# Taps in longer runs, parameter tables in memory, one addition by transfer

## The chip, the cores and the metric

One core of a Trainium2 chip. The metric is the device time of one execution in microseconds (us); 792.45 is the median of three runs of the kernel before.

## What is computed

Softmax attention with 32 heads of width 16 over 2048 positions, a long convolution whose taps come from a complex state space model, and a gate between the two:

```python
a = softmax(q k^T * 16**-.5) v @ wo              # per head, q, k, v = x @ wqkv
K = einsum("dn,dnl,dn->dl", C, exp(dt*A*l), dt*B).real   # 512 channels, 128 modes, 2048 taps
b = causal_conv(x, K) + x * Dskip
out = g * a + (1 - g) * b                        # g = sigmoid(sum(x * gate_w))
```

## The kernel before

The program of every engine is written out by a planner in Python. It knows a cost for each operation and a landing time for each transfer (`c`, `lat`, and a margin `DMARG` = 1.2 us on transfers), runs a model clock for each engine (`tm`), and lets threads (generators such as `params`, `tables`, `kgen`, `cloads`, `convs`, `projs`, `gate`) put their next operation in when it is ready by that model; a lower number is a higher priority. Each engine then does its list strictly in that order and waits on semaphores where a tile isn't there yet.

**Attention sets the beat.** The 2048 score tiles (128 keys by 512 queries) come in 683 groups of three. TensorE forms a group's scores in one of two PSUM banks (`SC`), ScalarE takes the exponential into `ET` (`ex`, line 949), TensorE multiplies by the values into `OA` (`pv`). A block is one head's 512 queries, 16 quads of four tiles; 32 blocks. Everything else is put in around this.

**VectorE takes tiles over.** In some groups ScalarE does two tiles and VectorE the third by bit arithmetic (`bits`, line 985; `batch`, line 996; tiles `DZ`, `DU`). Four such groups make a set. When sets may be taken is written in constants: the first window `WIN` opens at group 206 with four key positions of a block (`VKT`), the second at group 400 with seven, and none is taken before the mark "tabs" (`DVQ`), which is set when the last table is done; after it each set must find 0.3 us of modelled idle time of VectorE.

**Taps.** `params` makes complex powers of the modes and from them factors for two tables. For each of eight units `w` of 64 channels `tables` makes a left table `AT` (2 x 32 x 64 per mode) and a right table `PL` (2 x 112 x 64), both by doubling: copy a base, then `cmul` (two products and an addition) twice, and for `PL` six products with the factors `FF`. `AT`, `PL` and the eviction target `Ks` have two buffers each; a unit's tables wait for the mark `kg` of the unit two back. `kgen(w)` multiplies the tables on TensorE into the PSUM bank `MB` (2 x 128 matmuls of a 32-wide stationary operand), VectorE evicts to `Ks` (line 1240), and SP stores to `kd` in device memory. `MB` is under a lock that `kgen`, `projs`, `gate`, `convs`, `turn` and `outs` share.

**Convolution.** `cloads` loads for each of 32 channel groups the taps `WT` (four transfers; each partition reads a shifted stretch, in runs of 512 B) and the input `U`; `convs` does 128 matmuls with 32 columns of `WT` as the stationary operand, 16 elements apart; VectorE evicts (`Ys`), `turn` transposes by matmuls with `sel`. After the convolutions `outs` projects and writes out. `PACE` raises the priority of `convs` when they are behind a straight line from group 235 to 620.

Of the kernel before, what the change touches and what calls it, by code (L numbers as in the profile page):

```python
# [28 lines left out]
NPAD = 16  # L29
VB = (S + NPAD) * 16  # L30
# [24 lines left out]
NPL = 2  # L55
NPSEM = 8
# [3 lines left out]
CLAT = "tabs"  # L60
# [23 lines left out]
POW = (1, 2, 4, 8, 16, 32, 48, 256, 512, 1024)  # L84
# [373 lines left out]
def declare(nc, es):  # L458
# [58 lines left out]
    sb("AB", 7 * 2 * D)  # L517
    sb("BS", 4 * 2 * D)
    for m in (4, 8, 512, 1024):
        sb(f"F{m}", 3 * D)  # L520
    sb("FF", 3 * 3 * D)
    for k in range(2):
        sb(f"AT{k}", 2 * 32 * 64)
    for k in range(NPL):
        sb(f"PL{k}", 2 * 112 * 64)
    sb("ct1", 2 * 16 * 64)
# [112 lines left out]
def record(nc, p, B, ins):  # L639
# [426 lines left out]
    def fmul(o, n, x, xk, y, yk, yat=0, conj=False, at=0, t=("pt1", "pt2"), st=2 * D):  # L1066

        o, x, y, t1, t2 = B[o], B[x], B[y], B[t[0]], B[t[1]]
        c1, c2 = dv(2 * n * D), dv(n * D)
        pl = [[1, D]] if n == 1 else [[2 * D, n], [1, D]]  # L1070
        for tb, part in ((t1, 0), (t2, 1)):
# [5 lines left out]
        tt("DVE", lambda: o(at, [[1, D]] if n == 1 else [[st, n], [1, D]]), lambda: t1(0, pl), lambda: t2(D, pl), ALU.subtract, [(t1, 0), (t2, 0)], W, c2)  # L1077
        yield ("DVE", c2)
        if conj:
            op("DVE", lambda v: v.scalar_tensor_tensor(o(at + D, [[1, D]] if n == 1 else [[st, n], [1, D]]), t1(D, pl), -1.0, t2(0, pl), ALU.mult, ALU.subtract),  # L1080
               [(t1, 0), (t2, 0)], W, c=c2)
        else:
            tt("DVE", lambda: o(at + D, [[1, D]] if n == 1 else [[st, n], [1, D]]), lambda: t1(D, pl), lambda: t2(0, pl), ALU.add, [(t1, 0), (t2, 0)], W, c2)

    def factor(o, x, xk, at=0, xat=0, conj=False):

        o, x = B[o], B[x]
        yield ("DVE", .6)
        op("DVE", lambda v: v.tensor_copy(o(at, [[1, 2 * D]] if conj else [[2 * D, 2], [1, D]]), x(xat, [[1, 2 * D]] if conj else [[D, 2], [1, D]])), xk, [(o, at)], c=.6)
        yield ("DVE", .4)  # L1090
        op("DVE", lambda v: v.tensor_scalar(o(at + (2 * D if conj else D), [[1, D]]), x(xat + D, [[1, D]]), -1.0, None, ALU.mult), xk, [(o, at)], c=.36)

    def params():
        LA, AB, ZW, BS = B["LA"], B["AB"], B["ZW"], B["BS"]
# [19 lines left out]
        yield from fmul("BS", 2, "ZW", zk, "L2", key("L2"), at=4 * D, t=("LT1", "LT2"))  # L1114
        yield ("DVE", 1.15)
        op("DVE", lambda v: v.tensor_copy(BS(0, [[1, 4 * D]]), ZW(0, [[1, 4 * D]])), zk, [(BS, 0)], c=1.15)
        for m in (4, 8):
            yield from square(f"L{m}", f"L{m // 2}")
            yield from factor(f"F{m}", f"L{m}", key(f"L{m}"))
        for k, m in enumerate((16, 32)):  # L1120
            yield from square(f"L{m}", f"L{m // 2}")
            yield from factor("FF", f"L{m}", key(f"L{m}"), 3 * D * k)
        yield from fmul("L48", 1, "L16", key("L16"), "L32", key("L32"))
        yield from factor("FF", "L48", [(B["L48"], (0, "m"))], 6 * D)
        sch.mark("B")
        yield from square("LA", "L32", 0, 0)
# [12 lines left out]
        for m in (512, 1024):
            yield from square(f"L{m}", f"L{m // 2}")  # L1140
            yield from factor(f"F{m}", f"L{m}", key(f"L{m}"), conj=True)
        sch.mark("A")

    AT, PL, ct1 = [B["AT0"], B["AT1"]], [B[f"PL{k}"] for k in range(NPL)], B["ct1"]
# [4 lines left out]
    def ones():  # L1149
        yield ("AFTER", "g40")  # L1150
        for k in range(2):
# [7 lines left out]
    def cmul(x, xk, xs, N, o, W, f, fk, fat, m, ch):  # L1159

        n = 2 * m * ch
        c = hv(n)
        at = (N - 2 * m) * ch
        yield ("DVE", c)
        tt("DVE", lambda: ct1(0, [[m * ch, 2], [ch, m], [1, ch]]), lambda: x((N - m) * ch, [[xs, 2], [ch, m], [1, ch]]),
           lambda: f(fat, [[0, 2], [0, m], [1, ch]]), ALU.mult, xk + fk, [(ct1, 0)], c)
        yield ("DVE", c)
        tt("DVE", lambda: o(at, [[xs, 2], [ch, m], [1, ch]]), lambda: x(xs + (N - m) * ch, [[-xs, 2], [ch, m], [1, ch]]),
           lambda: f(fat + D, [[D, 2], [0, m], [1, ch]]), ALU.mult, xk + fk, W, c)
        yield ("DVE", c)  # L1170
        tt("DVE", lambda: o(at, [[xs, 2], [1, m * ch]]), lambda: ct1(0, [[m * ch, 2], [1, m * ch]]), lambda: o(at, [[xs, 2], [1, m * ch]]),
           ALU.add, [(ct1, 0)] + W, W, c)

    def tables():
        AB, BS, FF = B["AB"], B["BS"], B["FF"]
        yield ("AFTER", "A")
        for w in range(8):
            at, pl, d0 = AT[w % 2], PL[w % NPL], CH * w
            if w >= 2:
                yield ("AFTER", f"kg{w - 2}")  # L1180
            yield ("DVE", .35)
            op("DVE", lambda v, at=at, d0=d0: v.tensor_copy(at(24 * CH, [[AN, 2], [CH, 7], [1, CH]]), AB(12 * D + d0, [[D, 2], [-2 * D, 7], [1, CH]])),
               [(AB, 0), (AB, 1), (AB, (8 * D, "m"))], [(at, 0)], c=.35)
            ak = [(at, "one"), (at, 0)]
            for m, n in ((8, 512), (16, 1024)):
                f = B[f"F{n}"]
                yield from cmul(at, ak, AN, 32, at, [(at, m)], f, [(f, 0)], d0, m, CH)
                ak = ak + [(at, m)]
            if w == 0:
                yield ("AFTER", "B")  # L1190
            if w >= NPL:
                yield ("AFTER", f"kg{w - NPL}")
            if w == 1:
                yield ("AFTER", PLAT)
            yield ("DVE", .35)
            op("DVE", lambda v, pl=pl, d0=d0: v.tensor_copy(pl(60 * CH, [[PN, 2], [CH, 4], [1, CH]]), BS(6 * D + d0, [[D, 2], [-2 * D, 4], [1, CH]])),
               [(BS, 0), (BS, (4 * D, "m"))], [(pl, 0)], c=.3)
            pk = [(pl, 0)]
            for m, n in ((4, 4), (8, 8)):
                f = B[f"F{n}"]  # L1200
# [464 lines left out]
```

## Time and profile before

| | us |
|---|---|
| runs | 790.75, 792.45, 793.37 (median 792.45) |
| profiled execution | 790.26 |
| its span, first to last instruction | 788.5 |
| ScalarE (ACT) busy | 764.4 (97%) |
| TensorE (PE) busy | 706.7 (90%) |
| VectorE (DVE) busy | 698.6 (89%) |
| first AT copy / last PL product starts / first DZ | 118.6 / 286.5 / 291.9 |
| convolution matmuls, first and last start | 357.2 and 706.9 |

How to read the lines of the profile: a group row has the source line, engine, operation, tiles as written<-read with their shapes, the count, then busy us, mean ns of one, and after the second bar the idle time in front of them and what ended it. PEld is TensorE's weight load. A row of windows has the stretch, its length, each engine's busy time with its instructions in brackets, the clock granted to TensorE, the share of the DMA engines and GB/s. SPq is SP's queue of transfers; a row of transfers has the count, the size of each and the median time from issue to landing.

### The profile page before, as it was taken

To read this page: it belongs to the slowest core of one execution; us is meant where nothing else is said; L and a number is where in the kernel's file an instruction comes from. 1 tells how busy PE (TensorE), PEld (TensorE's weight loads), DVE (VectorE), ACT (ScalarE), POOL (GpSimd) and SP (SyncE) were. 2 spreads that over 40 slices of the span, in tenths; PEclk is the share of its full clock that TensorE was granted. 3 is DMA by queue.
4 is the path that set the end of the run, shared out by engine and by line. 5 is a ranking of instruction groups with operands and counts; after the bars stand their busy time and mean duration, and the time that the engine had idled before them with its cause. 6 is when DMAs were issued, how large, how long until landed. Compare 5 with 4: busy or idle time off the path is not lost.

```text
span 788.5 us, 31097 instructions
## 1 busy us (share of the span) xinstructions
PE 706.7 (90%) x14262; PEld 323.0 (41%) x14262; DVE 698.6 (89%) x1078; ACT 764.4 (97%) x694; POOL 11.9 (2%) x21
## 2 busy tenths in 40 slices
PE   6778777899899989999999999999999999998996
PEld 2323322454454544434444444444444444442221
DVE  5799999999899978878797988999989999999995
ACT  5999999999999999999999999999999999999995
POOL 4000000000000000000000000000000000000000
PEclk8999999999999999999999999999999999999999
DMA  9463000000100036003665555477554556304011
GB/s 213 84 127 63 9 5 20 24 25 26 30 25 26 26 100 162 13 19 86 171 176 157 150 160 166 143 196 207 159 163 131 145 167 173 88 7 124 32 35 35
DMA packets 125923, 76.22 MB, mean 97 GB/s; under 512 B 34240, under 2 KB 116576, under 8 KB 125792
## 3 DMA queue, kind: packets, MB, share of 16 engines
q1 hardware_dynamic: 123776, 73.05, 35.1%
q8 instruction: 112, 1.84, 1.0%
q10 hardware_dynamic: 2016, 1.18, 0.7%
q14 instruction: 19, 0.16, 0.1%
HBM read 59.12 MB, written 10.63 MB: 88 GB/s over the span
## 4 chain that ended last, share of the span: by engine, by line
ACT 84%; PE 12%; DVE 2%; POOL 1%; issue 1%; ACTq 0%; POOLq 0%
ACT ET L949 84%; PE SC L655 5%; PE OA L655 4%; PE MB L655 3%; POOL VE L723 1%; DVE DZ L985 1%; DVE OT L1020 0%; DVE DZ L996 0%; DVE Ys L1331 0%; ACT fo L1627 0%; DVE sel L1305 0%; DVE KT L749 0%; DVE YJ L1353 0%; ACT ea L1098 0%; DVE OnT L1039 0%
## 5 line engine op out<-in xcount | busy, mean ns | idle before, releaser
L949 ACT ACTIVATE ET<-SC 128x1024 bf16<-128x1024 f32 (+1 forms) x683 | 756.4, 1456 | 6.3 <-PE SC L655 5.1
L655 PE MATMUL SC<-Qm,KT 32*128 32x512 bf16 x2048 | 277.9, 385 | 63.8 <-ACT ET L949 58.7
L985 DVE TENSOR_SCALAR DZ<-SC 128x512 uint16<-128x512 f32 x384 | 255.8, 684 | 41.4 <-PE SC L655 38.9
L655 PEld LDWEIGHTS SC<-Qm,KT 32*128 32x128 bf16 x2048 | 71.4, 91 | 244.7 <-ACT ET L949 209.7
L655 PE MATMUL OA<-ET,VE 128*32 128x512 bf16 x1664 | 166.0, 391 | 0.2 <-ACT ET L949 0.2
L655 PE MATMUL OA<-wm 128*32 128x512 bf16 (+3 forms) x742 | 156.8, 366 | 1.7 <-DVE wm L706 1.2
L655 PEld LDWEIGHTS MB<-U,WT 128*32 128x32 bf16 x4096 | 91.4, 153 | 32.3 <-issue 22.6
L655 PE MATMUL MB<-U,WT 128*32 128x128 bf16 (+7 forms) x4096 | 103.3, 229 | 1.5 <-issue 1.5
L655 PEld LDWEIGHTS OA<-ET,VE 128*32 128x32 bf16 x1664 | 42.5, 93 | 93.2 <-issue 91.7
L996 DVE TENSOR_SCALAR DZ<-DZ 128x2048 uint16<-128x2048 uint16 x96 | 65.6, 683 | 7.9 <-PE OA L655 7.7
L655 PE MATMUL MB<-PL,AT 128*32 128x64 bf16 (+1 forms) x2048 | 68.9, 278 | 0.1
L996 DVE TENSOR_SCALAR DU<-DZ 128x2048 uint16<-128x2048 uint16 x96 | 64.5, 685 | 0.5
L655 PEld LDWEIGHTS MB<-PL,AT 128*32 128x32 bf16 x2048 | 56.1, 139 | 11.5 <-issue 5.7
L1043 DVE TENSOR_TENSOR PL<-PL,FF 128x2048 bf16<-128x2048 bf16 x48 | 56.2, 1217 | 0.3
L655 PEld LDWEIGHTS OA<-wm 128*32 128x32 bf16 (+2 forms) x742 | 40.3, 97 | 9.1 <-issue 7.3
L655 PE MATMUL OA<-DZ,VE 128*32 128x512 bf16 x384 | 38.0, 386 | 0.0
L655 PE MATMUL OA<-DZ,VS 128*32 128x512 bf16 x384 | 37.8, 383 | 0.0
L655 PE MATMUL OA<-DU,VS 128*32 128x512 bf16 x384 | 37.7, 383 | 0.0
L1020 DVE STREAM_TRANSPOSE OT<-OA 128x512 f32<-128x512 f32 x32 | 22.7, 709 | 5.2 <-PE OA L655 5.1
L1331 DVE CAST Ys<-MB 128x512 bf16<-128x512 f32 x32 | 21.7, 679 | 0.4 <-PE MB L655 0.2
L655 PE MATMUL MB<-Wv,xT 128*32 128x128 bf16 x1024 | 19.4, 219 | 0.0
L655 PEld LDWEIGHTS MB<-Wv,xT 128*32 128x32 bf16 x1024 | 16.7, 97 | 4.0 <-issue 1.1
(133 smaller groups left out, 449.2 us busy)
## 6 DMA issues: line engine op xcount, KB each, us to landing
WT<-gm_kd SPq DMA_DIRECT2D x128, 256.0 KB, 3.5
U<-gm_xr SPq DMA_DIRECT2D x32, 288.0 KB
U<-gm_xr SPq DMA_DIRECT2D x32, 284.0 KB
gm_xr<-Xp SPq DMA_DIRECT2D x4, 576.0 KB, 5.5
gm_kd<-Ks SPq DMA_DIRECT2D x32, 64.0 KB, 1.6
gm_yn<-YJ SPq DMA_DIRECT2D x2, 1024.0 KB, 4.8
Yl<-gm_yn SPq DMA_DIRECT2D x2, 1024.0 KB, 10.6
gm_qd<-Qs SPq DMA_DIRECT2D x15, 128.0 KB, 1.7
```

Of the source, the lines that this page charges most:

```text
L655: op("PE", lambda t: t.matmul(out(), lhsT(), rhs(), start=start, stop=stop, skip_group_check=True, **kw), R, W, c=c, lat=.15, a=a, cfg=cfg)
L723: op("POOL", lambda g, pi=pi: g.memset(VE(pi * 4 * VG, [[1, 4 * VG]]), 1.0), [(idb, 0)], [(VE, (pi, k)) for k in range(16)], c=2.3)
L949: op("ACT", lambda a: a.activation(ET(512 * e, [[1, 512 * n]]), sc(0, [[1, 512 * n]]), AF.Exp, scale=DH ** -0.5), [(sc, i, g) for i in ran ...
L985: op("DVE", lambda v: v.tensor_scalar(z.u16(512 * k, [[1, 512 * n]]), sc(512 * na, [[1, 512 * n]]), XS, XB, ALU.mult, ALU.add), [(sc, na + ...
L996: op("DVE", lambda v: v.tensor_scalar(t.u16(0, [[1, 2048]]), z.u16(0, [[1, 2048]]), float(STEP[k][0]), None, ALU.add), R, W, c=.07 + 2048 ...
L1020: op("DVE", lambda v: v.transpose(OT(512 * w, [[1, 512]]), OA(0, [[1, 512]])), [(OA, 0, b)], [(OT, w, b)], c=.64)
L1043: op(eng, lambda v: v.tensor_tensor(o(), a(), b_(), f), R, W, c=c)
L1331: op("DVE", lambda v_, ys=ys: v_.tensor_copy(ys(64, [[YW, NT // 4], [1, NJ]]), MB(0, [[NJ, NT // 4], [1, NJ]])), ky, [(ys, 0, x)], c=.62)
```

## The change

- **Taps.** The split of the tap index over the two tables is turned round: `AT` now steps by 4 up to 124, `PL` by 1 within 4 and then by 128. `kd` then holds for each tap modulo 128 a row of 16 x 16 elements, `WT`'s four transfers read runs of 2 KB, and the 32 columns of a stationary operand lie 128 elements (256 B) apart instead of 16 (32 B). `kgen` stores 16 more rows for each channel group, shifted by one (32 more transfers, of 4 partitions).
- **Parameter tables.** `params` writes into `PA` and `PB`, laid out by unit. `pstore` stores both to device memory (`pp`), in three transfers each: unit 0, unit 1, units 2 to 7. `aloads` and `ploads` load each unit's factors into `FU` (two buffers) and the bases straight into `AT` and `PL`, four transfers a unit from SP; VectorE's two copies a unit are gone. The order of `params` changes: what `AT` needs comes first.
- **One addition.** In `AT`'s second doubling (m = 16) the addition is made by a transfer from POOL's queue that accumulates `ct` into `AT`.
- `tables` becomes two threads, `atables` and `ptables`, with a product tile `ct` each; `kgen(w)` waits for both.

`WIN`, `DVQ`, `VKT`, `PACE` and the priorities of the other threads stay.

```diff
-VB = (S + NPAD) * 16
+VB = (P + 16) * 256
+UW = 43 * 64
+UA, UF, UB, UG = 0, 14 * 64, 20 * 64, 28 * 64
+DADD = (16,)
+ALAT0 = 2.6
+ALATM = .21
...
+        if m in DADD:
+            yield ("POOL", 1.0, 0)
+            dma("POOL", lambda e: e.dma_start(o(at, [[xs, 2], [1, m * ch]]), ct(0, [[m * ch, 2], [1, m * ch]]), accum_op=ALU.add),
+                [(ct, 0), (o, m, (sl, "h"))], [(o, m, sl)], c=1.0, lat=ALAT0 + m * ALATM)
...
+    def pstore():
+        for k, (b, lo, R) in enumerate(parts):
+            m = b.free // 8
+            yield ("AFTER", "AB"[k])
+            for w0, n in ((0, 1), (1, 1), (2, 6)):
+                yield ("SP", .6)
+                dma("SP", ..., c=.6, lat=2.5 + n * 1.6)
+    def uload(k, w, b, at, dims, src, n, W):
+        yield ("SP", .6)
+        dma("SP", ..., c=.6, lat=3)
+    def aloads():
+        for w in range(8):
+            at, fu = AT[w % NAT], FU[w % NFU]
+            if w >= NFU:
+                yield ("AFTER", f"pl{w - NFU}")
+                yield ("AFTER", f"at{w - NFU}")
+            yield from uload(0, w, fu, 0, [[1, UB - UF]], UF, UB - UF, [(fu, 0, w)])
+            yield from uload(1, w, fu, UB - UF, [[1, UW - UG]], UG, UW - UG, [(fu, 1, w)])
+            if w >= NAT:
+                yield ("AFTER", f"kg{w - NAT}")
+            yield from uload(0, w, at, 24 * CH, [[AN, 2], [1, 7 * CH]], UA, 7 * CH, [(at, 0, w)])
+    def ploads():
+        for w in range(8):
+            pl = PL[w % NPL]
+            if w >= NPL:
+                yield ("AFTER", f"kg{w - NPL}")
+            if w:
+                yield ("AFTER", f"pa{w - 1}")
+            yield from uload(1, w, pl, 60 * CH, [[PN, 2], [1, 4 * CH]], UB, 4 * CH, [(pl, 0, w)])
...
-            op("DVE", ... v.tensor_copy(ks(8 * b, [[16, 64], [1, 8]]), MB(0, [[1, 64], [64, 8]])), ky, [(ks, b, w)], c=.62)
+            op("DVE", ... v.tensor_copy(ks(8 * b, [[16, 16], [256, 4], [1, 8]]), MB(0, [[4, 16], [1, 4], [64, 8]])), ky, [(ks, b, w)], c=.62)
...
+            yield ("SP", .6, 2)
+            dma("SP", lambda e, j=j: e.dma_start(kd.dram((4 * w + j) * VB + P * 256, [[1024, 4], [256, 4], [1, 240]]), ks(16, [[256, 4], [1, 240]], 32 * j, 4)),
+                [(ks, 0, w), (ks, 1, w)], [(kd, ("x", 4 * w + j))], c=.6, lat=3)
...
+                    bigload(lambda e, n=n, i=i, wt=wt, v=v: e.dma_start(wt(n * i, [[1, n]]), kd.dram(v * VB + n * i, [[256, P], [1, n]])),
...
-                           lambda g=g, c=c, wt=wt: wt(512 * (nb - 1 - g) + NT * hf + c, [[16, 32]]),
+                           lambda g=g, c=c, wt=wt: wt(16 * (nb - 1 - g) + NT * hf + c, [[128, 32]]),
...
-                   ... (tables(), 2), ...
+                   ... (pstore(), 1), (aloads(), 1), (ploads(), 1), (atables(), 2), (ptables(), 2), ...
```

More of the change, by code (lines that the diff above doesn't have):

```diff
@@ L55 @@
 NPL = 2
+NAT = 2
+NKS = 2
+NFU = 2
+DADD = (16,)
+ALAT0 = 2.6
+ALATM = .21
 NPSEM = 8
@@ L516, in declare @@
     sb("ZW", 2 * 2 * D, FP32)
[L517 to L522, printed above, removed]
+    sb("PA", 8 * UB)
+    sb("PB", 8 * (UW - UB))
+    for k in range(NFU):
+        sb(f"FU{k}", 21 * 64)
+    for k in range(NAT):
         sb(f"AT{k}", 2 * 32 * 64)
@@ L1113, in params @@
         zk = [(ZW, 0), (ZW, (2 * D, "m"))]
[L1114 to L1126, printed above, removed]
+        yield from fmul("PB", 2, "ZW", zk, "L2", key("L2"), at="B", t=("LT1", "LT2"), dst=(64, 256))
+        for k in range(2):
+            yield ("DVE", .6)
+            op("DVE", lambda v, k=k: v.tensor_copy(PB(256 * k + 192, [[-64, 2], [UW - UB, 8], [1, 64]]), ZW(D * k, [[2 * D, 2], [64, 8], [1, 64]])), zk, [(PB, ("B", k))], c=.6)
@@ L1139, in params @@
-        for m in (512, 1024):
+            op("DVE", lambda v, x=x, n=n, e=e: v.tensor_scalar(PA(UA + 448 + 64 * e, [[-64, n], [UB, 8], [1, 64]]), x(D, [[2 * D, n], [64, 8], [1, 64]]), -1.0, None, ALU.mult),
+               xk, [(PA, ("A", e, 1))], c=c)
+        for m in (32, 64):
             yield from square(f"L{m}", f"L{m // 2}")
-            yield from factor(f"F{m}", f"L{m}", key(f"L{m}"), conj=True)
+            yield from factor(f"L{m}", key(f"L{m}"), UF + 192 * (m // 64), conj=True)
         sch.mark("A")
-    AT, PL, ct1 = [B["AT0"], B["AT1"]], [B[f"PL{k}"] for k in range(NPL)], B["ct1"]
+        for m in (128, 256):
+            yield from square(f"L{m}", f"L{m // 2}")
+            yield from factor(f"L{m}", key(f"L{m}"), UG - UB + 192 * (m // 256))
@@ L1145, in record @@
+        for k, m in enumerate((512, 1024)):
+            yield from square(f"L{m}", f"L{m // 2}")
+            yield from factor(f"L{m}", key(f"L{m}"), UG - UB + 192 * (2 + k))
+        yield from fmul("L1536", 1, "L512", key("L512"), "L1024", key("L1024"))
+        yield from factor("L1536", [(B["L1536"], (0, "m"))], UG - UB + 192 * 4)
+        sch.mark("B")
+    AT, PL = [B[f"AT{k}"] for k in range(NAT)], [B[f"PL{k}"] for k in range(NPL)]
     CH = 64
@@ L1150, in ones @@
         yield ("AFTER", "g40")
-        for k in range(2):
+        for k in range(NAT):
             yield ("POOL", .4)
@@ L1181, in tables @@
[L1181 to L1188, printed above, removed]
@@ L1189, in tables, with ptables @@
-            if w == 0:
-                yield ("AFTER", "B")
+            at, fu = AT[w % NAT], FU[w % NFU]
+            if w >= NAT:
+                yield ("AFTER", f"kg{w - NAT}")
+            ak = [(at, "one"), (at, 0, w)]
+            for i, m in enumerate((8, 16)):
+                yield from cmul(B["ctA"], at, ak, AN, 32, at, w, fu, [(fu, 0, w)], 192 * i, m, CH)
+                ak = ak + [(at, m, w)]
+            sch.mark(f"at{w}")
+    def ptables():
+        yield ("AFTER", "B")
+        for w in range(8):
+            pl, fu = PL[w % NPL], FU[w % NFU]
@@ L1191, in tables @@
             if w >= NPL:
                 yield ("AFTER", f"kg{w - NPL}")
[L1193 to L1200, printed above, removed]
-                yield from cmul(pl, pk, PN, 64, pl, [(pl, m)], f, [(f, 0)], d0, m, CH)
-                pk = pk + [(pl, m)]
@@ L1203, in tables @@
-            fk = [(FF, 3 * D * k) for k in range(3)]
+            pk = [(pl, 0, w)]
+            for i, m in enumerate((4, 8)):
+                yield from cmul(B["ctP"], pl, pk, PN, 64, pl, w, fu, [(fu, 1, w)], UB - UF + 192 * i, m, CH)
+                pk = pk + [(pl, m, w)]
+            fk, f0 = [(fu, 1, w)], UB - UF + 384
+            sch.mark(f"pa{w}")
             for lo, n in LAST:
@@ L1533, in record @@
     for th, pr in ((norms(), 0), (qms(), 0), (projs(), 1), (gth, 1.1), (params(), 2), (vscaled(0), 2.2), (vscaled(1), 2.2), (relay(), 4),
-                   (ones(), 4), (zeros(), 4), (tables(), 2), (cloads(), 3), (convs(), 2), (outs(), 1.5)):
+                   (ones(), 4), (zeros(), 4), (pstore(), 1), (aloads(), 1), (ploads(), 1), (atables(), 2), (ptables(), 2), (cloads(), 3), (convs(), 2), (outs(), 1.5)):
         if th is gth:
```

112 lines of the change are left out of this document (62 added, 50 removed).

## The prediction

> **What bounds the kernel now.** I read the page's first, second and fourth part, then the groups with shapes kept apart, then the stages.
>
> ```profile
> span 788.5 us, 31097 instructions
> PE 706.7 (90%) x14262; PEld 323.0 (41%) x14262; DVE 698.6 (89%) x1078; ACT 764.4 (97%) x694; POOL 11.9 (2%) x21
> ACT  5999999999999999999999999999999999999995
> ...
> ACT 84%; PE 12%; DVE 2%; POOL 1%; issue 1%; ACTq 0%; POOLq 0%
> ...
> L949 ACT ACTIVATE ET<-SC 128x1024 bf16<-128x1024 f32 (+1 forms) x683 | 756.4, 1456 | 6.3 <-PE SC L655 5.1
> ```
>
> ScalarE (ACT) is the bound: 97% busy, 84% of the chain that ended last, and nearly all of it is one line, the exponential of 683 groups of score tiles. Only two things change the time: how many tiles ScalarE must do, and how long it is kept waiting. Of the second there is little: 6.3 us in front of all exponentials.
>
> The first is set by VectorE (DVE), which takes one tile of three off ScalarE in some groups. Two windows of ScalarE, before the first such group and after, and VectorE around that point:
>
> ```profile
> L949 ACT ACTIVATE ET<-SC 128x1536 bf16<-128x1536 f32 x206 | 276.9, 1937 | 0.4 <-PE SC L655 0.4
> ...
> L949 ACT ACTIVATE ET<-SC 128x1024 bf16<-128x1024 f32 x154 | 147.2, 1156 | 2.9 <-PE SC L655 2.7
> L949 ACT ACTIVATE ET<-SC 128x1536 bf16<-128x1536 f32 x47 | 67.4, 1572 | 0.5 <-PE SC L655 0.4
> ...
> 264.19 0.68 DVE L1240 CAST Ks<-MB 128x512 bf16<-128x512 f32 x1
> ...
> 268.96 0.38 DVE L1182 COPY AT<-AB 128x896 bf16<-128x896 bf16 x1
> ...
> 285.34 2.35 DVE L1043 TENSOR_TENSOR PL<-PL,FF 128x2048 bf16<-128x2048 bf16 x2
> 287.61 1.90 DVE L971 TENSOR_SCALAR VS<-VE 128x608 bf16<-128x608 bf16 x8
> 291.94 0.69 DVE L985 TENSOR_SCALAR DZ<-SC 128x512 uint16<-128x512 f32 x1 [2.44 <-PE SC L655]
> ```
>
> The reader is to see three things. Exactly 206 groups of full width (1.344 us each) run before the first narrow one, and 206 is the lower bound of the first window in `WIN`, which the change leaves alone. The tables end 4.3 us ahead of it (the last PL product at 285.3 to 287.7, the first DZ at 291.94). And from there to 500 us, 154 of 201 groups are narrow: 77%, the share that four keys of a block of 16 allow (16 of 21.3 groups is 75%), so that stretch lacks keys, not VectorE time. A narrow group saves (1.344 - 0.924) = 0.42 us, where 0.924 is (756.4 - 298 x 1.344) / 385 narrow ones; a set is four of them, 1.7 us.
>
> The stages, VectorE alone in the eight units of the tables (first and sum), then all engines:
>
> ```profile
> 118.50:143.10 24.60, 22.93 (x32) 1.00 0.08 26
> ...
> sum 169.20, DVE 155.68; mean DVE 19.46
> ...
> core 0: us, PE busy (x) PEld busy (x) DVE busy (x) ACT busy (x) POOL busy (x), PEclk, DMA share, GB/s
> ...
> 300.00:340.00 40.00, 39.96 (x655) 18.27 (x655) 32.41 (x53) 38.45 (x39) 0.00 (x0) 0.96 0.27 74
> 340.00:500.00 160.00, 149.87 (x3443) 72.80 (x3443) 135.86 (x226) 158.14 (x157) 0.00 (x0) 1.00 0.51 140
> 500.00:775.00 275.00, 258.17 (x4952) 110.96 (x4956) 259.01 (x425) 272.51 (x276) 0.00 (x0) 1.00 0.44 123
> ```
>
> A unit takes 21.15 us, 19.46 of them busy on VectorE. ScalarE is full through this stage (its digits are 9), so the tables do not lie on the path; their end does, if it slips past the opening of the window. Behind 500 us VectorE is 94% busy (259.01 of 275), and there it is what limits the sets.
>
> **The change part by part.** The sum is made against the profiled execution: 790.26 us, of which 788.5 is the span. The median of the runs shown is 792.45, 2.2 above; the prediction is given on the median's scale, so 2.2 is added at the end. About 0.3% (2.4 us) is what a measurement of this kernel can tell from no change.
>
> ```profile
> L1043 DVE TENSOR_TENSOR PL<-PL,FF 128x2048 bf16<-128x2048 bf16 x48 | 56.2, 1217 | 0.3
> L1043 DVE TENSOR_TENSOR AT<-ct,AT 128x2048 bf16<-128x2048 bf16 x8 | 9.8, 1220 | 0.2
> L1043 DVE TENSOR_TENSOR PL<-ct,PL 128x1024 bf16<-128x1024 bf16 x8 | 5.5, 692 | 0.3
> L1043 DVE TENSOR_TENSOR PL<-ct,PL 128x512 bf16<-128x512 bf16 x8 | 3.4, 424 | 0.2
> L1182 DVE COPY AT<-AB 128x896 bf16<-128x896 bf16 x8 | 3.1, 384 | 0.0
> L1196 DVE COPY PL<-BS 128x512 bf16<-128x512 bf16 x8 | 2.3, 286 | 0.0
> ...
> Yl<-gm_yn SPq DMA_DIRECT2D x2, 1024.0 KB, 10.6
> gm_qd<-Qs SPq DMA_DIRECT2D x15, 128.0 KB, 1.7
> ...
> gm_yn<-YJ SPq DMA_DIRECT2D x1, 1024.0 KB, 4.8
> Qm<-gm_qd SPq DMA_DIRECT2D x1, 16.0 KB, 4.4
> ...
> WT<-gm_kd SPq DMA_DIRECT2D x128, 256.0 KB, 3.5
> ```
>
> *VectorE work.* Removed: eight last additions (1.220) and sixteen copies (0.384, 0.286), 8 x 1.89 = 15.1 us. Added in `params`: a few conversions split in two or three, about 0.5 us. It is worth nothing by itself: it lies before group 206, where ScalarE has no tile to give away. Its cover is that bound; gone is the cover only if the tables end after about 290.
>
> *The spill and the loads by unit.* Today the first AT copy follows `params` at once. Now `pstore` writes the second part (1472 elements x 2 B x 128 x 8 units = 2944 KB) and the AT base of unit 0 is queued behind it, since `aloads` loads the factors of both parts first. The last rows price this. A Qm load issued 0.6 us behind a 1024 KB store landed 4.4 us later, with the store; so one queue serves in order. Store against store, (1024 - 128) KB took 4.8 - 1.7 = 3.1 us, 289 KB/us. So 2944 KB take 10.2 us, 1.6 more for the landing, and two loads of 240 and 224 KB about 1.6 plus a landing of 1.6 (less where they overlap): the base lands 14 us after `params`. The kernel's own order assumes 11.3 (0.6 + 4.1 + 1.2 for the store, two issues at 0.6, 3 + 1.2 for the load with its margin, and 0.6). VectorE then waits some 2.5 us longer than planned, and what stands behind the waiting multiply (a Qs or VE eviction, a norm) waits too, and with it TensorE and then ScalarE. Ends: 0, if no eviction that TensorE needs stands there, and 14, if the store runs at the rate of the 1024 KB load (10.6 us). I take +1.0, near the store's row, half covered by ScalarE's two banks.
>
> The Trainium skill's page "SBUF — State Buffer", section "The DMA setup-cost knee", fits a transfer as 2 us plus its bytes at 436 GB/s. As an estimate by that page the 3.0 MB take 8.9 us, the base lands at about 11, no wait is left, and the sum below would be 1.0 us less; the store's row has it slower.
>
> *The pace of the units.* VectorE-bound, a unit falls from 21.15 to about 19.3. But a table now begins with a load that may start only when the unit two back is done: today the last eviction of unit 5 ends at 264.9 and the AT copy of unit 7 starts at 268.96, 4.1 us later; a load of 256 KB lands in 3.5 and the kernel allows 4.8. That eats between none and half of the gain. I take 1.1 us a unit (ends -0.7 and 1.9): eight units give back 9 (ends -6 and 15). The late start takes 14, less some 6 us of evictions that can fill it: unit 0's stretch is busy 22.93 us, of which the table itself is 17 (6 x 1.217, 3 x 1.220, 6 x 0.69, 3 x 0.42 and the copies). The tables then end near 287, with 281 and 301 as ends: about where they end now. One slot of a set lost behind group 206 costs 1.7 us; I take a third of one, +0.5.
>
> *POOL's eight accumulating transfers.* No row shows one. Nearest are 1.7 (128 KB store) and 10.6 us (1024 KB load) to landing; the kernel counts 6.0 and a margin of 1.2. What hides it is the PL table of the same unit, 6 x 1.217 and six smaller products, over 10 us of VectorE before `kgen` reads AT. Cost 0; beyond about 11 us every microsecond is paid up to eight times. POOL's queue holds nothing else there.
>
> *SP's queue.* 38 spill and unit transfers and 32 tail stores come in, each 0.3 to 0.6 us to issue like the rows of this queue; between 119 and 345 us it has about that many already and stands idle most of the time. A block's Qm loads are issued a block, 28 us, ahead, so 10 us behind a spill don't reach TensorE. Cost 0.
>
> *Taps in 2 KB runs.* The 128 WT loads land in 3.5 us today and no matmul's wait is put down to them; faster ones are hidden anyway: 0. What they change on TensorE is the step of the weight columns, 32 to 256 bytes.
>
> ```profile
> L655 PEld LDWEIGHTS MB<-gwT,xT 128*128 128x128 bf16 x48 | 1.6, 96 | 1.4 <-issue 1.4
> ...
> L655 PEld LDWEIGHTS MB<-gwT,xT 128*128 128x128 bf16 x64 | 4.6, 162 | 1.9 <-issue 1.7 <-DVE DZ L985 0.2
> ...
> L655 PEld LDWEIGHTS MB<-U,WT 128*32 128x32 bf16 x4096 | 91.4, 153 | 32.3 <-issue 22.6
> L655 PEld LDWEIGHTS MB<-PL,AT 128*32 128x32 bf16 x2048 | 56.1, 139 | 11.5 <-issue 5.7
> ```
>
> The gate's weights show that a step costs (96 ns adjacent, 162 at a step of 32 bytes), but AT's, at 128 bytes, take 139 ns against WT's 153 at 32: a longer step is no dearer. I take 0; ends -1 and +3 (a tenth of WT's 91.4 us is 9 us over 365, in a stage where TensorE idles 10 of 160).
>
> *Convolutions.* They may start a little earlier or later with the tables. One of them is about 0.7 + 0.35 us of VectorE; moved from behind 500 us to before it, it buys a quarter of a set: -0.3.
>
> Sum: +1.0 + 0.5 - 0.3 = +1.2. The dip of TensorE's clock in 300 to 340 (0.96, ScalarE 38.45 of 40, 1.5 us lost) may go or come back elsewhere: a third of it, -0.5. Net +0.7: 791.0 on the profile's scale, 793 on the median's.
>
> **The rivals.** *Tables too late, slower.* If the unit is bound by the load behind `kgen` (gain -0.7 a unit) the tables end near 300, two slots and more of sets are lost (3.4 to 4 us), and the first wait adds 1 to 2.5: 798. For it speaks the 4.1 us row, against it that projections may fill the idle start and leave `MB` freer later.
>
> *The accumulate lands late, slower.* At 13 us from issue, 2 us of TensorE standing in `kgen`, eight times, half of it ScalarE's: about +8, 801. It decides from 11 us on. The rows bound it only by 10.6. The Trainium skill ("SBUF — State Buffer", "A bandwidth-pool intuition that's wrong") says that a POOL-issued transfer waits while VectorE runs a two-port copy or tensor_scalar on SBUF; no run here shows it yet.
>
> *Faster.* The tables end at 281 to 284, `kgen` of the last unit and the gate stop crowding 288 to 340, the clock dip goes (-1.5), two or three convolutions move ahead of 500 us (-1), and one set more comes out: -3 to -4, 789. For it speaks the 15.1 us; against it, that nothing before group 206 can use them.
>
> **How the numbers follow.** No change beyond 0.3%: 0.45, at 793. Tables too late 0.20 at 798, late accumulate 0.13 at 801, faster 0.22 at 789. So faster 0.22, same 0.45, slower 0.33. The range takes in the faster case and the bulk of both slower ones: 787.5 to 801; the likeliest's own is 790 to 795.
>
> **What would show it.** First narrow group still after 206 full ones; narrow ones near 385; the last PL product between 281 and 292; a wait of VectorE on a transfer of 10 us or more around 120 to 133; kgen's matmuls without a wait on AT; WT weight loads near 150 ns; no wait on WT. Wrong would make it: a count of narrow groups other than 377 to 393, ScalarE idle between 100 and 290, or weight loads of WT well over 160 ns.

## The result, and the profile after

The changed kernel takes 820.05 us (median of 4 runs, 817.92 to 824.96), the kernel before 791.60 (4 runs, 790.33 to 793.37): 1.037 times the time before, interval 1.031 to 1.042. The profiled execution took 818.44 us, 28.2 more than that of before. The forecast was 793 us, no change, with a range of 787.5 to 801.

The page after: the span, the busy times, ScalarE's slices, the chain that ended last, the exponentials, the convolutions' weight loads and matmuls, and two rows of the DMA issues.

```profile
span 816.6 us, 31206 instructions
...
PE 740.0 (91%) x14270; PEld 366.9 (45%) x14270; DVE 703.4 (86%) x1051; ACT 790.5 (97%) x694; POOL 20.8 (3%) x29
...
ACT  5999999999999999999999999999999999999995
...
ACT 56%; PE 27%; DVE 11%; DMA 3%; POOL 1%; issue 1%; DVEq 0%; ACTq 0%; SPq 0%; POOLq 0%
...
L956 ACT ACTIVATE ET<-SC 128x1024 bf16<-128x1024 f32 (+1 forms) x683 | 782.6, 1395 | 8.0 <-PE SC L662 6.2
...
L662 PEld LDWEIGHTS MB<-U,WT 128*32 128x32 bf16 x4096 | 134.5, 203 | 24.1 <-issue 20.7
L662 PE MATMUL MB<-U,WT 128*32 128x96 bf16 (+7 forms) x4096 | 138.7, 256 | 0.9 <-issue 0.7
...
L662 PEld LDWEIGHTS MB<-PL,AT 128*32 128x32 bf16 x2048 | 55.2, 137 | 9.8 <-issue 5.7
...
WT<-gm_kd SPq DMA_DIRECT2D x128, 256.0 KB, 3.7
...
AT<-ctA POOLq DMA_DIRECT2D x8, 512.0 KB, 5.3
```

One row stands out: the loads of WT take 203 ns each instead of 153, 134.5 us instead of 91.4, while AT's stay as they were. TensorE's share of the chain has gone from 12% to 27%, ScalarE's from 84% to 56%. Yet ScalarE still reads 97% busy, with nines in every slice. Its busy time does not show where it was slowed; the number of its instructions per window does. The exponentials (ET) alone in the two late windows, the kernel before first, the changed one second; columns are PE, PEld and ACT busy with counts, clock, DMA share and GB/s:

```profile
340.00:500.00 160.00, 34.83 (x348) 8.95 (x348) 158.14 (x156) 1.00 0.51 140
500.00:775.00 275.00, 58.78 (x596) 15.19 (x596) 272.51 (x276) 1.00 0.44 123
```

```profile
340.00:500.00 160.00, 33.45 (x332) 8.93 (x332) 158.42 (x148) 1.00 0.36 115
500.00:775.00 275.00, 55.55 (x556) 14.48 (x556) 271.31 (x258) 1.00 0.41 128
```

The same busy time holds 148 groups instead of 156, and 258 instead of 276: 1.07 us of busy time a group against 1.01, and 1.05 against 0.99. The single record does not get longer; over all groups its mean is even shorter, 1395 ns (above) against 1456 in the kernel before. But a record starts while the one before it still runs, and that overlap shrinks: for the narrow groups from 340 to 500 us the records overlap by 0.23 us on average in the kernel before and by 0.14 in the changed one, and from one end to the next it takes 0.94 and 0.99 us (worked out from both traces). So the late scores show as less overlap, and hardly as idle time of ScalarE.

Where the 28 us arise follows from the n-th exponential's start in the one trace against its start in the other (worked out from both traces; us later than before):

```
group (start before)     60     88     190    270    290    350    430    510    590    650
                        (96)  (133)  (271)  (359)  (379)  (443)  (524)  (605)  (684)  (744)
changed                 1.3    3.1    2.5    2.1    2.7    6.3   12.0   18.1   25.6   26.6
```

About 2 us come in at 123 to 133 us, where the tables begin; then nothing up to 379 us, although the first two of the 32 convolutions run at 316 to 341 us already; then a steady 24 us while the other thirty run. From group 650 to the end it is 1.4 us more.

The tables' end and the first groups are as forecast. Of the changed kernel, the groups before and behind the window's opening, then VectorE around it:

```profile
L956 ACT ACTIVATE ET<-SC 128x1536 bf16<-128x1536 f32 x206 | 277.3, 1771 | 2.5 <-PE SC L662 2.4
...
L956 ACT ACTIVATE ET<-SC 128x1024 bf16<-128x1024 f32 x153 | 151.3, 1130 | 1.9 <-PE SC L662 1.3
L956 ACT ACTIVATE ET<-SC 128x1536 bf16<-128x1536 f32 x47 | 68.9, 1558 | 0.0
```

```profile
287.81 1.22 DVE L1050 TENSOR_TENSOR PL<-PL,FU 128x2048 bf16<-128x2048 bf16 x1
...
294.46 0.69 DVE L992 TENSOR_SCALAR DZ<-SC 128x512 uint16<-128x512 f32 x1 [2.34 <-PE SC L662]
```

Again 206 full groups come first, and the last PL product ends at 289.0.

### The profile page after: what moved, and what is told of

It is laid out like the page before. It is cut to its first block, busy times and chain, and to the rows that moved or that the text cites. A ratio compares the mean times of both kernels' runs of the same rounds, so it can differ in the third digit from the quotient of the medians.

```text
span 816.6 us, 31206 instructions
## 1 busy us (share of the span) xinstructions
PE 740.0 (91%) x14270; PEld 366.9 (45%) x14270; DVE 703.4 (86%) x1051; ACT 790.5 (97%) x694; POOL 20.8 (3%) x29
## 4 chain that ended last, share of the span: by engine, by line
ACT 56%; PE 27%; DVE 11%; DMA 3%; POOL 1%; issue 1%; DVEq 0%; ACTq 0%; SPq 0%; POOLq 0%
ACT ET L956 56%; PE MB L662 11%; PE SC L662 9%; PE OA L662 7%; DVE DZ L992 3%; DMA AT<-gm_pp 1%; DVE pt L1050 1%; POOL VE L730 1%; DMA gm_yn<-YJ 1%; DMA Yl<-gm_yn 1%; DVE L L1050 1%; DVE Ys L1391 1%; DVE KT L756 1%; DVE OT L1027 1%; DVE L L1071 0%
## 5 line engine op out<-in xcount | busy, mean ns | idle before, releaser
L956 ACT ACTIVATE ET<-SC 128x1024 bf16<-128x1024 f32 (+1 forms) x683 | 782.6, 1395 | 8.0 <-PE SC L662 6.2
L662 PE MATMUL OA<-wm 32*128 32x512 bf16 (+3 forms) x758 | 158.0, 364 | 1.2 <-DVE wm L713 1.2
L662 PEld LDWEIGHTS MB<-U,WT 128*32 128x32 bf16 x4096 | 134.5, 203 | 24.1 <-issue 20.7
L662 PE MATMUL MB<-U,WT 128*32 128x96 bf16 (+7 forms) x4096 | 138.7, 256 | 0.9 <-issue 0.7
L1003 DVE TENSOR_SCALAR DZ<-DZ 128x2048 uint16<-128x2048 uint16 x95 | 74.5, 785 | 9.9 <-PE OA L662 9.8
L1003 DVE TENSOR_SCALAR DU<-DZ 128x2048 uint16<-128x2048 uint16 x95 | 72.0, 766 | 0.4
L1050 DVE TENSOR_TENSOR PL<-PL,FU 128x2048 bf16<-128x2048 bf16 (+1 forms) x64 | 64.9, 1051 | 0.2
L1027 DVE STREAM_TRANSPOSE OT<-OA 128x512 f32<-128x512 f32 x32 | 25.2, 788 | 9.3 <-PE OA L662 8.0
L1050 DVE TENSOR_TENSOR ctA<-AT,FU 128x1024 bf16<-128x1024 bf16 (+1 forms) x16 | 15.3, 954 | 8.3 <-DMA AT<-gm_pp 8.2
```

Of the source, the lines that this page charges most:

```text
L662: op("PE", lambda t: t.matmul(out(), lhsT(), rhs(), start=start, stop=stop, skip_group_check=True, **kw), R, W, c=c, lat=.15, a=a, cfg=cfg)
L956: op("ACT", lambda a: a.activation(ET(512 * e, [[1, 512 * n]]), sc(0, [[1, 512 * n]]), AF.Exp, scale=DH ** -0.5), [(sc, i, g) for i in ran ...
L1003: op("DVE", lambda v: v.tensor_scalar(t.u16(0, [[1, 2048]]), z.u16(0, [[1, 2048]]), float(STEP[k][0]), None, ALU.add), R, W, c=.07 + 2048 ...
L1027: op("DVE", lambda v: v.transpose(OT(512 * w, [[1, 512]]), OA(0, [[1, 512]])), [(OA, 0, b)], [(OT, w, b)], c=.64)
L1050: op(eng, lambda v: v.tensor_tensor(o(), a(), b_(), f), R, W, c=c)
```

## The experiments

Each ratio is against runs of the kernel before that were taken beside the experiment; their medians are 788.9 to 791.0 us.

**The weight step.** First the two kernels with their steps exchanged, then other steps, all in the convolutions' `lhsT`. Code is cut to the part that changes.

Changed kernel, 32 bytes:

```
-  wt(16 * (nb - 1 - g) + NT * hf + c, [[128, 32]])
+  wt(512 * (nb - 1 - g) + NT * hf + c, [[16, 32]])
```

> The changed kernel with one thing undone: the convolutions read the 32 columns of a stationary operand 16 elements (32 B) apart again, at the offsets of the kernel before; loads, tables, order and counts stay, so the taps are taken from the wrong places. Theory W (the 256 B step of the weight columns makes each group of four matmuls take about 93 ns instead of 62, and TensorE then holds ScalarE up): WT weight loads back to 153 ns, 203 before, and the time to 793 to 797, the rest of the change being worth +2 to +5. Rival D (something else of the change slows the convolutions: 2 KB runs written into SBUF beside them, or the changed order of work): WT weight loads stay near 200 ns and the time near 820.

```profile
L662 PEld LDWEIGHTS MB<-U,WT 128*32 128x32 bf16 x4096 | 92.5, 152 | 31.5 <-issue 21.9
```

794.43 us, 1.006 of before (1.003 to 1.010). The loads are back at 152 ns and four matmuls at 62 ns from start to start (medians from the trace), against 91 to 95 in the kernels with 256 bytes. Of the 28 us, all but some 5 are gone with this one line.

Kernel before, 256 bytes (`[[16, 32]]` becomes `[[128, 32]]`, with 16 in place of 512):

> The kernel before with one thing of the change alone: the 32 columns of a stationary operand of the convolutions 128 elements (256 B) apart, at the changed kernel's offsets; the taps are then taken from the wrong places. Theory W: WT weight loads about 200 ns, time 813 to 820. Rival D: 153 ns and 792.

```profile
L655 PEld LDWEIGHTS MB<-U,WT 128*32 128x32 bf16 x4096 | 132.6, 203 | 24.9 <-issue 20.7
```

817.90 us, 1.035 (1.030 to 1.041). The delay is 0.0 up to 270 us and grows by 23 us from group 290 to 650, as in the changed kernel (24). The 5.9 us in between are not the step's alone: 4 of them come in at 304 to 321 us, before the first convolution (361 us), where the granted clock is 0.5 in this execution. So the step by itself makes the loss of the convolutions' stage, in a kernel that has nothing else of the change.

Kernel before, 128 bytes (`wt(256 * ..., [[64, 32]])`):

> The kernel before with the columns 64 elements (128 B) apart (taps from the wrong places). If the cost grows with the distance between columns: weight loads near 175 ns and a time between 795 and 810. If it is a matter of 256 B alone (columns that fall on the same place of some period): 150 to 155 ns and 792, as AT's weight loads at the same step take 139.

```profile
L655 PEld LDWEIGHTS MB<-U,WT 128*32 128x32 bf16 x4096 | 120.5, 197 | 28.0 <-issue 20.7
```

803.66 us, 1.018 (1.010 to 1.025, from two runs): nearly the same load, where the expectation had 175 or 150 to 155 ns; some 90 ns for four matmuls; and half of the loss. From group 290 to 650 the delay grows by 13 us, against 23 with 256 bytes. TensorE is busy with these matmuls for 103.4 us in the kernel before, 128.9 with 128 bytes and 137.1 with 256: 25.5 and 33.8 us more, of which 12 and 11 don't show in the time. So an estimate from these rows is that about 11 us are covered by TensorE's spare time and the rest is paid. Why 128 bytes take 8 us less of TensorE than 256, at nearly the same median, was not tried.

Kernel before, 240 bytes (`wt(16 * ..., [[120, 32]])`):

> The kernel before with the columns 120 elements (240 B) apart (taps from the wrong places), nearly as far as in the changed kernel but no multiple of 64 B. If distance counts: weight loads near 200 ns and 812 to 820, as with 128 elements. If a period counts: 150 to 160 ns and 791 to 795.

```profile
L655 PEld LDWEIGHTS MB<-U,WT 128*32 128x32 bf16 x4096 | 90.7, 151 | 32.8 <-issue 22.9
```

789.45 us, 1.001 (0.998 to 1.004): a step almost as long as the slow one costs nothing. It is not the distance by itself.

Kernel before, 64 bytes (`wt(256 * ..., [[32, 32]])`):

> The kernel before with the weight columns of the convolutions 64 bytes apart (32 elements) where it has 32, so that the weights are other taps than the reference's; all else as before. So far 32 and 240 bytes give 62 and 61 ns for four matmuls of 32 columns, 128 and 256 bytes 91 and 92 ns. If what costs is that the step is a multiple of 64 bytes or more of a power of two, this one is slow in part or whole: loads 170 to 203 ns, four matmuls 75 to 92 ns, time 800 to 805 us. If it starts at 128 bytes, loads at 150 to 155 ns, four matmuls at 62 ns, time 788 to 791 us.

```profile
L655 PEld LDWEIGHTS MB<-U,WT 128*32 128x32 bf16 x4096 | 93.2, 154 | 34.2 <-issue 24.5
```

789.65 us, 0.998 (0.994 to 1.002). 64 bytes cost no more than 32; of the steps tried, 128 and 256 are the slow ones.

Kernel before, 256 bytes, the four side-by-side matmuls starting apart (`wt(16 * ((nb - 1 - g + 2 * j) % nb) + ...`):

> The kernel before with weight columns 256 bytes apart, but the four matmuls of a group, which run side by side on four strips of 32 columns of TensorE, start 64 bytes apart in a weight row instead of 2 bytes (so the weights are other taps than the reference's). If the price of the step comes from four loads side by side that read the same places of memory in the same order, as AT's loads don't (their four start 32 bytes apart and took 139 ns at 128 bytes): loads fall to 150 to 160 ns, four matmuls to 62 to 70 ns, time 789 to 795 us. If each load pays for its step by itself: 203 ns, 92 ns and 817 to 819 us, as without the offset.

```profile
L655 PEld LDWEIGHTS MB<-U,WT 128*32 128x32 bf16 x4096 | 133.1, 204 | 24.6 <-issue 20.7
```

816.89 us, 1.034 (1.025 to 1.042, from two runs). These other starts change nothing, which speaks against the idea that four loads clash in the same places; other offsets were not tried.

Changed kernel, padded: an unused element behind every 16 taps, so that rows are 272 elements and the step is 272 bytes. The cuts below are the main ones; the stores of `kgen` and the loads of `WT` follow the same rows.

```
+RW = 16 * 17
-VB = (P + 16) * 256
+VB = (P + 16) * RW
...
-  ks(8 * b, [[16, 16], [256, 4], [1, 8]])
+  ks(8 * b, [[17, 16], [RW, 4], [1, 8]])
...
-  wt(16 * (nb - 1 - g) + NT * hf + c, [[128, 32]])
+  wt(17 * (nb - 1 - g) + NT * hf + c, [[136, 32]])
```

> The changed kernel with one unused element behind every 16 taps: rows of 272 elements instead of 256 in gm_kd, Ks and WT, so that the weight columns stand 272 bytes apart and runs are 2176 bytes; all results as the reference's. If the price lies in steps of 128 and 256 bytes, as the earlier runs show, and not in steps beyond some length: loads of WT at 150 to 155 ns, four matmuls at 61 to 63 ns, time 793 to 796 us, as with the step of 32 bytes in the changed kernel (794.4 against 788.9). If long steps cost in themselves: loads at 200 ns, time 815 to 820 us.

```profile
L663 PEld LDWEIGHTS MB<-U,WT 128*32 128x32 bf16 x4096 | 90.3, 149 | 29.5 <-issue 19.7
```

790.62 us, 1.001 (0.998 to 1.005) of before, under the 793 to 796 that were expected. With one element of padding per run the whole loss is gone. What is left of the change is nothing measurable here, as was forecast for it, and 1.006 (1.003 to 1.010) in the changed kernel with 32 bytes: between 0 and some 5 us. What makes 128 and 256 bytes dear, and whether other multiples of 128 are, no run shows.

**Why AT's row did not show it.** AT's weight columns stand 128 bytes apart too, in both kernels. Two runs, on the kernel with the spread stores (below), with 60 elements in place of 64, first for AT, then for AT and PL.

> The kernel with the spread stores, with AT's weight columns 120 bytes apart in the tables' matmuls where it has 128 (so the taps are other than the reference's). If AT's loads pay for the step of 128 bytes as WT's do: four matmuls of the tables fall from 87 and 113 ns to 60 to 80, TensorE is 10 to 20 us less busy in 150 to 300 us, and the loads' record falls well under 139 ns. If AT's step is free and the moving operand, whose columns stand 128 bytes apart too, sets the pace: 87 and 113 ns stay, the record at 135 to 140. The time stays within 2 us of the spread kernel's 787.9 either way, since ScalarE is full there.

> As the run before, with the moving operand's columns (PL) 120 bytes apart too. If the moving operand sets the pace of the tables' matmuls through its step of 128 bytes: four matmuls fall to 50 to 65 ns. If any step beyond adjacent columns costs the moving operand the same, or the number of columns sets it: 87 and 113 ns stay (or what the run before has). Time within 2 us of 787.9.

```profile
L663 PE MATMUL MB<-PL,AT 128*32 128x64 bf16 x1024 | 60.0, 290 | 0.2 <-DVE Qs L757 0.2
L663 PE MATMUL MB<-PL,AT 128*32 128x48 bf16 x1024 | 57.9, 263 | 0.0
L663 PEld LDWEIGHTS MB<-PL,AT 128*32 128x32 bf16 x2048 | 55.7, 141 | 10.4 <-issue 6.1 <-DVE Ks L1319 0.2 <-DVE PL L1051 0.2
```

```profile
L663 PE MATMUL MB<-PL,AT 128*32 128x64 bf16 x1024 | 65.6, 307 | 0.3 <-DVE Qs L757 0.2
L663 PE MATMUL MB<-PL,AT 128*32 128x48 bf16 x1024 | 63.1, 276 | 0.0
```

787.15 and 787.76 us, where the kernel they start from had 787.85. With AT at 120 bytes (first fence) four matmuls take 86 and 113 ns, as with 128 (87 and 113), and the load reads 141 ns instead of 137: nothing moved. With PL at 120 bytes too they take 95 and 126, slower, which neither theory had. So the step of the moving operand changes the pace of the tables' matmuls and that of their loads doesn't; a group takes 25 to 51 ns more than the convolutions' 62, and a load's price would have room behind it. Whether AT's loads pay for their 128 bytes there stays open.

**The start of the tables.** The 2 to 3 us at 123 to 133 us stayed with every step of the weights. VectorE's waits in the padded kernel, 118 to 150 us (total, times, longest), and its window from 120 to 160:

```profile
DVE VE L767 <- PE MB L663: 7.1, 3, 2.9
DVE ctA L1051 <- DMA AT<-gm_pp: 3.3, 1, 3.3
...
120.00:160.00 40.00, 29.89 (x569) 11.68 (x569) 30.55 (x44) 38.09 (x29) 2.53 (x2) 1.00 0.54 148
```

ScalarE loses 1.9 of 40 us. First arrangement: unit 0's AT base and left factors issued ahead of the stores of six units. (The 8.2 us that the next expectation names are all four waits on a base in the changed kernel's run; the one at the start of the tables is 2.9.)

```
             for w0, n in ((0, 1), (1, 1), (2, 6)):            # pstore
+                if (k, w0) in ((0, 2), (1, 0)):
+                    yield ("AFTER", "al0")
...
-            yield from uload(1, w, fu, ...)                   # aloads: right factors
             if w >= NAT:
+                yield from uload(1, w, fu, ...)
...
             yield from uload(0, w, at, ...)                   # the base
+            sch.mark(f"al{w}")
+            if w < NAT:
+                yield from uload(1, w, fu, ...)
```

> The padded changed kernel, with unit 0's loads of the left factors and of the AT base issued on SP's queue right behind the stores of units 0 and 1, ahead of the two stores of six units. If the wait on the AT base behind those stores (8.2 us of VectorE put down to it) is what costs 2 to 3 us at 122 to 134 us: that wait falls under 3 us, the delay of the groups against the kernel before at 134 us is under 1.5 us, and the time is 2 to 3 us under the padded kernel's, 790 to 793 us. If the loss there comes from elsewhere (the clock of TensorE, crowded projections), the delay stays at 2 to 4 us and the time within 1 us of the padded kernel's.

```profile
PEld OA L663 <- DVE OT L1028: 3.6, 1, 3.6
DVE ctA L1051 <- DMA AT<-gm_pp: 3.6, 1, 3.6
...
120.00:160.00 40.00, 30.29 (x590) 11.90 (x582) 26.09 (x38) 36.85 (x28) 1.39 (x2) 0.96 0.57 164
```

793.60 us, 1.004 (1.001 to 1.008), no gain. The delay at 133 us is gone (0.1), and at 144 us there are 4.0: the wait is now on unit 1's base, with the transposes of the attention's output queued behind it on VectorE, and TensorE's clock dips (0.96). Second arrangement: all that units 0 and 1 need ahead of both six-unit stores.

> The padded changed kernel with every store and load of units 0 and 1 (the AT bases, the factors, unit 0's PL base) ahead of the two stores of six units on SP's queue. With unit 0's base alone moved ahead the wait went on to unit 1: 3.6 us on its AT base at 135 us, with a transpose of the attention's output behind it, and a dip of the clock. If the stores of six units are what is late: the waits on AT from 115 to 140 us sum to under 2 us, VectorE is busy 30 us or more of 120 to 160, ScalarE 39.5 of these 40, the delay against the kernel before is under 1 us at 150 us, and the time 2 to 3 us under the padded kernel's, 786 to 789 us where before gives 789.5. If VectorE simply has nothing to do there but wait for projections, or the clock dips anyway: the delay stays at 2 to 4 us, and the time at 789 to 793.

```profile
DVE Qs L757 <- DMA gm_qd<-Qs: 3.5, 1, 3.5
PEld MB L663 <- DVE Qs L757: 3.0, 1, 3.0
...
120.00:160.00 40.00, 30.59 (x609) 12.14 (x605) 26.62 (x39) 37.48 (x29) 1.61 (x2) 0.96 0.69 213
```

792.44 us, 1.002 (0.999 to 1.005). No wait on a base is left; instead the store of a block's queries stands behind the stores, its buffer comes free late, and a projection waits 3.0 us for it. Third: the spill in single units, spread over the first unit's tables, with the bases and left factors of units 0 and 1 loaded first.

```
-for w0, n in ((0, 1), (1, 1), (2, 6)):
+for k, w0 in [(0, 0), (0, 1)] + [(0, w) for w in range(2, 8)] + [(1, w) for w in range(8)]:
...
+    if w0 > 1:
+        yield ("AFTER", ("al1", "pl0ld")[k])          # behind the bases / PL's base of unit 0
+        if k and w0 > 3:
+            yield ("AFTER", ("at0", "pa0")[w0 > 5])   # behind unit 0's tables
...
```

> The padded changed kernel with the spill cut into single units and spread: AT bases and left factors of units 0 and 1 right behind their stores, the other six of the first part one by one behind them, of the second part two at once, four with the first unit's tables, two behind its first PL products, so that no load or store of a block waits behind more than about 1.5 MB. With the base first, the wait went on to unit 1's base (3.6 us), with all small transfers first to the store of a block's queries (3.5 us). If it is the queue's bytes: no single wait of VectorE on a transfer over 2 us from 110 to 160 us, ScalarE 39.5 or more of 120 to 160, delay against the kernel before under 1 us at 170 us, time 787 to 790 us where before gives 789.5. If something else makes the stall (VectorE waits for the projections of VE in the same place): the delay stays at 2 to 4 us and the time at 789 to 793.

```profile
DVE VE L767 <- PE MB L663: 4.2, 3, 2.9
DVE ctA L1051 <- DMA AT<-ctA: 0.6, 1, 0.6
...
120.00:160.00 40.00, 32.41 (x736) 15.08 (x732) 32.64 (x43) 40.00 (x31) 1.81 (x2) 1.00 0.51 148
```

787.85 us, 0.995 of before (0.992 to 0.998). ScalarE is full from 120 to 160 us, and the delay there is 0.5 us, and 0.2 at 190. The three arrangements together put the loss down to the bytes of the spill on SP's queue: what stands behind the stores of six units (1920 and 2208 KB) is waited for 3 to 4 us, and it is a different transfer each time. The tables end at 282.1 us here, and VectorE takes 385 groups' third tile again, where the padded kernel has 381; by the prediction's 1.7 us a set, that is part of the gain. This version is faster than the kernel before by 0.5%, and its interval leaves out 1.

**VectorE's time before group 206.** The padded kernel with AT's last addition on VectorE (`DADD = ()`):

> The padded changed kernel with AT's last addition on VectorE again, eight of 1.22 us, and no accumulating transfer. If the transfer is hidden and VectorE's time ahead of group 206 is worth nothing: within 1 us of the padded kernel, 789 to 792 us, with the last PL product up to 10 us later than its 288.9 us. If those 10 us decide about the opening of the window: fewer than 381 narrow groups or VectorE late behind 292 us, 793 to 796 us. If the transfers of 512 KB disturb (a write and a read that VectorE, the weight loads or other transfers wait for): faster by 2 us or more, 786 to 788.

```profile
250.81 0.17 DVE L1451 COPY gp<-MB 128x12 f32<-128x12 f32 x1
...
267.34 0.17 DVE L1451 COPY gp<-MB 128x16 f32<-128x16 f32 x1 [5.58 <-PE MB L663]
...
304.68 0.17 DVE L1451 COPY gp<-MB 128x16 f32<-128x16 f32 x1
...
330.63 3.48 DVE L1051 TENSOR_TENSOR PL<-PL,FU 128x2048 bf16<-128x2048 bf16 x3
335.01 0.69 DVE L993 TENSOR_SCALAR DZ<-SC 128x512 uint16<-128x512 f32 x1 [0.89 <-PE SC L663]
```

815.04 us, 1.030 (1.025 to 1.035), which no theory had expected. The order written out for this kernel puts the gate (`gp`) between the tables, at 251 to 305 us, where the padded kernel has it behind them at 351; the tables end at 334, the first tile of VectorE comes at 335, and 365 narrow groups are left of 381. The clock is lower too: 0.969 on average over the six runs, against 0.989 beside them, and in the trace half clock from 255 to 272 us. So the run tells what late tables and a lower clock cost together, not what the addition costs. With the gate held behind the tables (`yield ("AFTER", "tabs")`):

> The padded changed kernel with AT's last addition on VectorE and the gate held behind the tables, where the changed kernel has it anyway. If the loss of 24 us with the addition on VectorE came from the gate between the units: tables end at 290 to 298 us instead of 288, first tile of VectorE by 298, 373 to 381 narrow groups, 790 to 795 us, and the accumulate is worth 0 to 4 us. If it came from the additions themselves (eight of 1.22 us in front of kgen): tables end beyond 310 us again and the time is over 800.

796.27 us, 1.007 (1.004 to 1.010), against 1.001 for the padded kernel. The tables end at 301.3 us instead of 288.9, later than the 290 to 298 that were expected, and the first tile comes at 302.0; 381 groups are narrow all the same. The difference of the two ratios, 0.5% or 4 us, is an estimate of what the accumulating transfers bring here: the two intervals overlap (1.004 to 1.010, 0.998 to 1.005), and the convolutions start later as well (the first one's result at 379 us instead of 323).

**The window earlier.** The kernel with the small transfers first, `WIN` opened at 198:

> As the kernel with the small transfers first, and with the window in which VectorE takes tiles opened at group 198 instead of 206, which makes 385 narrow groups instead of 381, one set of four more, as in the kernel before. If VectorE's time ahead of group 206 is worth something once the window opens earlier: a set is 4 x 0.42 = 1.7 us, time 784 to 788 us, 1.5 us under the same kernel with 206. If the tables, which end near 288 us, then collide with the first tiles of the set (group 198 starts near 283 us): the tables end later, the units of the convolutions start later, no gain or 1 to 3 us slower.

```profile
340.00:400.00 60.00, 57.49 (x781) 20.74 (x769) 39.14 (x62) 51.48 (x50) 0.00 (x0) 0.74 0.17 55
```

806.94 us, 1.021 (1.017 to 1.024), which neither theory had. The row is the stretch behind the tables: the granted clock is 0.74, and ScalarE is busy 51.48 of 60 us. The tables end at 288.9 us as before, so they did not collide; TensorE's clock was what was lost: it stands at 0.5 for about 31 us between 352 and 390. What in this order brings the clock down was not found, but the traces have a hint. In 13 of the 17 the clock falls to 0.5 for 3 to 31 us somewhere between 200 and 400 us, and in each of them such a stretch lies within the gate's matmuls (one moving column each) or within 2 us of them; only this run has one elsewhere too. Four traces, the changed kernel's among them, have the gate without it, so it is not shown as the cause.

## Why the prediction was wrong

**The step that failed** is the term for the weight columns: "AT's, at 128 bytes, take 139 ns against WT's 153 at 32: a longer step is no dearer. I take 0; ends -1 and +3". The step from 32 to 256 bytes costs 24 us by the delays in the convolutions' stage, 28 by the ratios (1.035 for the kernel before with the step alone; 1.037 for the changed kernel against 1.001 padded): the loads go from 153 to 203 ns, a group of four from 62 to some 93 ns, and 1024 groups times 31 ns are 32 us of TensorE in a stage that has some 10 of 160 to spare. Two errors lie in it. A price was carried over from AT's loads to WT's by the duration of a record: at the same 128 bytes AT's loads read 137 to 139 ns and WT's 197, and AT's groups go at 87 and 113 ns whether their step is 128 bytes or 120, so the row could not tell what a step costs where the loads set the pace. And the upper end was taken as a tenth of the loads' time without a row that bounded it; a step that no row shows, on 4096 loads in a stage where TensorE is 94% busy, has a bound of the size of the loads themselves. The prediction's list of what would make it wrong did name "weight loads of WT well over 160 ns"; the chance it gave that was none.

The Trainium skill's page "SBUF — State Buffer", section "Door 1: The DMA port swizzle", says that successive accesses are free only within a line of 16 bytes, eight bf16. By that rule all the steps tried here would cost alike; the runs have 149 to 154 ns at 32, 64, 240 and 272 bytes and 197 to 204 at 128 and 256, so the measurement decides: past one line it is not the distance that sets the price.

**The start of the tables** was taken as +1.0, with 14 as an end. It is 2 us in the changed kernel's profile (1.0 to 3.1) and 2.6 in the padded one's. The mechanism was right, the AT base behind the stores and VectorE with other work queued behind its wait: the wait ends at 130.0 us, 13 us after the last write to `PB`, where 14 were forecast. Three evictions of `VE` stand ahead of it, each with a wait of 2 to 2.9 us for TensorE, so the wait put down to the base is only 2.9 us, and the wait of 10 us or more that was named as a sign did not show. The cover by ScalarE's banks was overestimated.

**SP's queue**, taken as 0 because "10 us behind a spill don't reach TensorE", holds for the Qm loads but not for the queries' stores: when these stood behind the spill, in the second arrangement, VectorE waited 3.5 us and TensorE 3.0.

**The tables' pace and VectorE's time.** The tables end at 289.0 (forecast near 287; 281 to 292 as the sign), 206 full groups come first, 381 narrow ones follow (forecast near 385): one set fewer, 1.7 us. That VectorE's 15.1 us are worth nothing by themselves fits the condition that the prediction named, that the tables end before about 290. With the additions back on VectorE they end at 301, and some 4 us are lost, by two ratios whose intervals overlap.

**The accumulating transfers** land in 5.3 us by the median and 6.9 at most, where the kernel counts 6.0 and the prediction put the price beyond 11; `kgen` waits for none. **2 KB runs** land in 3.7 us against 3.5: no faster, and hidden, as forecast. **The rivals**: late tables came in the two runs that made them late (796 and 815 us, the second at a lower clock too), but not in the changed kernel; the late accumulate did not occur; the faster case, tables at 281 to 284 and one set more, came only after the spill had been spread (282.1 us and 385 narrow groups, 787.85 us).

## What to carry to other kernels

A new step of a strided weight operand is a term of its own: bound it by the loads' whole time, and if the new step is 128 or 256 bytes, the two that were slow here, price a padded row beside it (here one element in seventeen is worth 24 to 28 us). Read a weight load's price from the interval between groups in a stage where nothing else sets the pace, not from the duration of its record elsewhere. When a block of transfers is put on a queue, ask of everything behind it on that queue, not only of the first load that needs it, when it will land, and cut the block into pieces if several transfers are needed soon. Where records of an engine overlap, count them per stretch of time; the busy share can stay at 97% while the work slows down.

## What the hardware showed that was not expected

- Weight loads of 32 columns cost 149 to 154 ns at steps of 32, 64, 240 and 272 bytes and 197 to 204 ns at 128 and 256. With 256 bytes it made no difference whether the four loads of a group start 2 or 64 bytes apart.
- Between runs of one kernel the time follows the granted clock: over the 12 runs of the spread version, 784.6 us at a mean clock of 0.998 and 790.7 at 0.985, about 5 us for each 0.01. The base-first kernel, 1.004 of before, had a mean clock of 0.984 where before had 0.989; at equal clock (a line through each kernel's runs, read at 0.99) it has 790.3 and before 789.6, the spread version 788.1 against 790.7.
- Matmuls with 48 and 64 moving columns 128 bytes apart take 87 and 113 ns for four, more than the convolutions' 62 ns for 72 to 128 columns.
